# Score visits that own two pairs of PSUM banks instead of four adjacent ones, with a new fixed list

## The chip, the cores and the metric

The kernel runs on one core of one Trainium2 chip. A core has five engines with a queue each: TensorE (PE, matrix products into PSUM), ScalarE (ACT), VectorE (DVE), GpSimd (POOL) and SyncE (SP, which here only issues DMAs). The metric is the device time of one execution in microseconds; the profile is of one execution.

## The reference

The reference is one transformer block on 2048 tokens of 640 features, in bf16: an attention with a compressive memory, then a SiLU feed-forward of width 1728, both behind a LayerNorm without weights and with a residual. The attention has 32 heads of 20 features and works through four segments of 512 tokens:

```python
for s in range(N):                      # N = 4 segments, H = 32 heads
    logits = einsum('bhqd,bhkd->bhqk', qs, ks) * scale + mask      # causal
    a_dot = einsum('bhqk,bhkd->bhqd', softmax(logits), vs)
    pq = phi(qs)                        # t + 1 for t > 0, else exp(t)
    a_mem = einsum('bhld,bhde->bhle', pq, M) / (einsum('bhld,bhd->bhl', pq, z) + 1e-06)
    outs.append(g * a_mem + (1.0 - g) * a_dot)      # g = sigmoid(beta)
    M = M + einsum('bhld,bhle->bhde', phi(ks), vs)
    z = z + sum(phi(ks))
h  = x + concat(outs) @ wo
h2 = h + silu(layernorm(h) @ w1) @ w2
```

## The kernel before

**Tasks and a written list.** The kernel declares some 1,370 small tasks (a group of matmuls into PSUM, an eviction, an exponential, a DMA) with what each reads and writes. `ORDER` (L358) is one fixed list of all of them. `Graph.schedule` (L287) walks it and emits each task on its engine's queue in that order. An entry is `name/engine:slots`: the letter after the slash chooses ACT (A), DVE (D) or SP (S) where a task may run on more than one, and the numbers after the colon are the buffers that the task takes into use. `schedule` refuses a list in which a buffer is taken before its former owner's last user stands in the list. Every engine works strictly through its own part of the list. `Tracker.add` (L79) derives the semaphore waits from the data, so the list sets order and place, and the waits set the times. `fillN` entries are N matmuls on zeros.

**The names.** By segment s, head group g (4 heads, 8 groups), projection chunk c and token block b (128 tokens):
- `n1_st`, `n1_rs`, `n1_ap`, `n1_tr`: LayerNorm of a block (DVE statistics, POOL, DVE apply, DMA transpose issued by SP). The first four blocks are transposed on PE instead (`n1_tp`, evicted by `n1_te`).
- `re_wq`, `re_wk`: the loaded wq and wk are rearranged in SBUF by ACT or DVE.
- `v`, `ve`: value projection (L774) and eviction. `pr`, `qe`: projection of q or k (L808) and eviction. `ex`, `ph`: the two halves of phi. `vt`: twelve small DMAs of a segment that copy parts of q and k to other partitions (L844); the groups 5 to 7 need all of them.
- `qk`: the scores of one visit (L880), `e`: their exponentials (L891), `mk`: causal masks on POOL (L903), `av`: product with the values (L926), `oe`: its eviction (L939, L941), `tn`, `nm`, `ad`: transpose back together with the memory's term, normalisation on DVE, and sum of both parts on POOL.
- `kt`, `mz`, `ma`, `mb`: update of the memory M. `ot`, `wo`, `rs`: transpose of the attention's output by DMA, output projection (L1109), residual. `n2_*`: the second LayerNorm. `h1`, `th`, `s`: first feed-forward product (L1143; the last, narrow one L1138), tanh on ACT, product on DVE. `h2`, `o`, `out`: second product (L1178), residual, store.

The segments overlap: feed-forward and output work of one segment stand in the list among the scores of the next. PE's tasks use three tilings of the array: full, four row tiles (`qk`) and four column tiles (`av`; two in the narrow `h1`).

**PSUM.** The pool `ps` has the eight PSUM banks. A projection or `h1` takes one, a `v`, `wo`, `h2` or memory `tn` two neighbours. A score visit computes four heads at once, one bank each: 512, 384 or 256 + 256 columns. It takes four adjacent banks as one buffer, and two exponentials evict it, each two banks. The four banks come free together in the list, after the second exponential. In the list of before all visits use banks 4 to 7 or banks 0 to 3. The first matmul of a visit waits for everything that the visit needs.

Of the kernel before, what the change touches and what calls it, by code (L numbers as in the profile page):

```python
# [324 lines left out]
D = 640  # L325
# [38 lines left out]
pr020:2 ex001:0 qe021/A:0 e0x2:1 e0x0 qe020/A n1_st5:4 n1_st6:5 pr041:0 re_wq3/D av1x:3 qk2x0:4 w_wo/S:0  # L364
x8/A:8,9,10,11 vt06:0 vt00 vt03 vt09 qe041/D:0 pr031:1 pr030:0 n1_st4:6 n1_st7:7 w_w1_0/A:0 mk0x e2x2:0 oe1x/D:0
e2x0 ex041:1 qe030/D:0 qk0yb0:4 pr040:2 w_w1_1/S qe031/A qe040/D mk2x e0yb2:0 e0yb0 n1_rs5 av2x:0 av0x:3 tn1x:1
nm1x:0,0 oe0x/A:1 mk0yb n1_rs6 mtb1 qk1yb0:4 vt010 oe2x/D:0 vt08 vt05 vt02 vt07 vt04 e1yb2:1 e1yb0 ex021:2 zf0 v03:2
# [12 lines left out]
pr111:0 qe121/D:0 e6ya0:0 e6ya2 qk6yb0:4 qe120/D ex121:2 av5y:3 n2_tr0 h1_0_7_0:1 h1_0_0_0:2 e6yb2:0 e6yb0 qk7ya0:4  # L380
th0_7_0:0 ph101:2 qe111/D:0 oe5y/D:0 tn4y:0 s0_7_0:0 th0_0_0:1 h1_0_8_0:3 nm4y:0 s0_0_0 mz01:1 mz04:0 ma01/D:2
h1_0_3_0:2 e7ya2:1 e7ya0 th0_8_0:0 ma04/D:3 s0_8_0 th0_3_0:1 s0_3_0 tn5y:1 qk7yb0:4 e7yb2:1 mk6yb e7yb0 mk7yb mta0
av6y:0 mtb0 oe6y/A:1 h1_0_12_0:3 h1_0_1_0:2 qk8a0:4 th0_1_0:0 e8a2:0 e8a0 th0_12_0:1 s0_1_0 pr110:0 nm5y:1 qe110/D
h1_0_10_0:2 av7y:1 qk8e0:4 oe7y/D:0 th0_10_0:0 s0_12_0 pr130:0 s0_10_0 e8e2:0 e8e0 h1_0_5_0:2 h1_0_11_0:3 qk8b0:4
th0_5_0:1 n1_ap8:3 qe130/D:0 th0_11_0:0 w_w2_2/S kt03:1 tn7y:0 s0_5_0 nm7y:2 mz03:1 s0_11_0 h1_0_2_0:2 e8b2:0 e8b0
ma03/D:4 h1_0_6_0:0 th0_2_0:1 h1_0_13_0:1 th0_13_0:0 qk9a0:4 pr131:3 s0_2_0 s0_13_0 n1_ap10:0 h1_0_4_0:1 h1_0_9_0:2
qe131/D e9a2:1 e9a0 mk8a mk8e mm0 th0_6_0:1 th0_4_0:0 ex100:1 s0_6_0 mm4 mk8b mm6 qk9b0:4 vt19:0 th0_9_0:1 mm2 mm8
n1_rs9 mtb2 s0_4_0 w_w2_3/S vt16 vt10 vt18 e9b2:1 e9b0 av8:3 h2_0_0:0 h2_0_1 qk10a0:4 s0_9_0 ph100:0 ex141:1 ph121:1
e10a2:0 e10a0 h2_0_2 tn6y:2 h2_0_3 ph141:0 ex120:2 mk9a qk10b0:4 oe8/D:0 nm6y:3 o0 mzc0 mzc6 ph120:0 mzc2 h2_1_0:2
mk9b mm10 mzc4 e10b0:0 kt10:0 vt15 mm1 mzc1 mb00:0 e10b2 mk10a mzc5 mzc8 mm7 mzc7 mb03:0 mk10b ex111:1 n1_tr10:0  # L390
tn8:0 vt11 n1_tr8 nm8:0,0 h2_1_1 vt13 ot2 ot3 qk10e0:4 ph111:2 vt111 kt12:1 vt17 vt110 vt12 h2_1_2 av9:0 h2_1_3
# [24 lines left out]
n1_rs12 n1_ap12:2 ma23 n1_st13:6 e20e2:0 e20e0 th1_7_0:0 h1_1_11_0:2 qk21a0:4 h1_1_5_0:3 ad16 n1_rs14 mk20a s1_7_0
n1_ap14:1 s1_2_0 h1_1_6_0:1 e21a0:1 e21a2 n1_rs13 th1_11_0:0 mk20e n1_ap13:0 mk21a n1_tr12:0 v30:4 n1_tr13 n1_tr14
# [36 lines left out]
def build(nc, es, A_x, A_wq, A_wk, A_wv, A_wo, A_beta, B_x, B_w1, B_w2, out):  # L454
    T = Tracker()
# [396 lines left out]
    def declare_ticks(s):  # L852
# [10 lines left out]
        def scores(name, pool, pt, blocks, pr, width=L, sub=WH):  # L863
# [392 lines left out]
```

## Time and profile before

| what | value |
|---|---|
| median of 3 runs | 306.86 us (306.14 to 307.66) |
| profiled execution | span 305.4 us, its only time on record; the median is 1.46 us above it |
| instructions | 7240 |
| busy PE / ACT / DVE / POOL | 291.0 / 227.0 / 218.7 / 143.5 us |
| exponentials of scores (L891) | 168, 156.2 us busy between 19 and 250 us |
| ACT idle before L891, waiting for L880 | 14.3 us in 25 places |
| mean granted clock of TensorE | 0.994 |

An engine that is busy for the largest share need not be the one that sets the end in every stretch. The kernel has three: a start that waits for weights (to about 18 us), the attention's segments with everything else woven in (to about 250 us), and a tail of feed-forward products (to the end). A line of a group gives source line, engine, operation, tiles, shapes and count, then busy time and mean, then the idle time just before it and what ended that. `SPq` or `ACTq` is that engine's queue issuing a DMA, `PEld` the loading of a matmul's stationary operand.

### The profile page before, as it was taken

What the parts mean: (1) busy time and instruction counts of PE and PEld (TensorE: products, weight loads), DVE (VectorE), ACT (ScalarE), POOL (GpSimd) and SP (SyncE); (2) the same over time, 40 slices, a digit from 0 to 9 for tenths busy, and PEclk for the clock granted to TensorE, in tenths of its full rate; (3) what the DMA queues carried; (4) which work ended last, traced back from release to release, by engine and by line L of the source; (5) the groups of instructions that cost most, each with busy time, mean ns of one, the idle gap of its engine ahead of it and who ended that gap; (6) DMA issues with size and microseconds to landing.
All of it is one profiled execution on the core that took longest, in us unless ns stands there. A gap on an engine that the chain in (4) does not pass through costs nothing.

```text
span 305.4 us, 7240 instructions
## 1 busy us (share of the span) xinstructions
PE 291.0 (95%) x2876; PEld 166.5 (55%) x2900; DVE 218.7 (72%) x490; ACT 227.0 (74%) x322; POOL 143.5 (47%) x280
## 2 busy tenths in 40 slices
PE   8699898999999999999999999999999999999996
PEld 6434454555655445656654444556564466764574
DVE  5567999796788895877989878449776476934523
ACT  4488998999998979989889899978878951004410
POOL 4227754433687856536747419334973730300000
PEclk9899999999999999999999999999999999999999
DMA  6658468642264040055552400034250004242001
GB/s 197 211 195 239 75 166 223 127 97 42 90 105 80 17 62 2 1 91 76 114 146 63 67 17 19 2 64 69 39 108 2 0 2 88 64 88 86 0 24 64
DMA packets 48578, 24.65 MB, mean 81 GB/s; under 512 B 38881, under 2 KB 47457, under 8 KB 48545
## 3 DMA queue, kind: packets, MB, share of 16 engines
q1 hardware_dynamic: 47872, 23.09, 33.1%
q10 hardware_dynamic: 672, 1.10, 1.1%
q8 instruction: 23, 0.38, 0.5%
q14 instruction: 11, 0.08, 0.1%
HBM read 10.41 MB, written 2.62 MB: 43 GB/s over the span
## 4 chain that ended last, share of the span: by engine, by line
PE 72%; ACT 12%; DVE 7%; DMA 4%; issue 2%; POOL 1%; SPq 1%; DVEq 0%; ACTq 0%
PE ps_all L1178 18%; PE ps_all L1143 16%; PE ps_all L808 12%; PE ps_all L1109 7%; PE ps_all L880 6%; PE ps_all L926 5%; ACT PTA L891 4%; ACT PTB L891 3%; DMA sT<-in_A_wq_dram 3%; PE ps_all L774 2%; PE ps_all L955 2%; ACT PTE L891 2%; DMA oT<-otok 1%; PE ps_all L959 1%; PE ps_all L1048 1%
## 5 line engine op out<-in xcount | busy, mean ns | idle before, releaser
L891 ACT ACTIVATE PTA<-ps_all 128x1024 bf16<-128x1024 f32 x64 | 62.1, 1027 | 7.1 <-PE ps_all L880 6.5
L1178 PE MATMUL ps_all<-w_sb,sT 128*128 128x320 bf16 x448 | 65.2, 299 | 0.0
L891 ACT ACTIVATE PTB<-ps_all 128x1024 bf16<-128x1024 f32 (+1 forms) x64 | 58.9, 970 | 5.9 <-PE ps_all L880 5.6
L1143 PE MATMUL ps_all<-hT,w_sb 128*128 128x512 bf16 (+1 forms) x315 | 60.1, 335 | 0.9 <-issue 0.5
L1152 ACT ACTIVATE th<-ps_all 128x512 f32<-128x512 f32 (+2 forms) x70 | 34.0, 507 | 34.5 <-PE ps_all L1143 26.8
L1158 DVE SCALAR_TENSOR_TENSOR sT<-th,ps_all 128x512 bf16<-128x512 f32 (+2 forms) x70 | 38.0, 561 | 26.1 <-ACT th L1152 25.0
L903 POOL TENSOR_SCALAR_AFFINE_SELECT PTB<-PTB 128x512 bf16<-128x512 bf16 x64 | 41.2, 644 | 32.7 <-ACT PTB L891 30.4
L1178 PEld LDWEIGHTS ps_all<-w_sb,sT 128*128 128x128 bf16 x448 | 42.3, 98 | 19.3 <-issue 2.1
L1143 PEld LDWEIGHTS ps_all<-hT,w_sb 128*128 128x128 bf16 x325 | 30.3, 98 | 23.9 <-issue 1.3
L891 ACT ACTIVATE PTE<-ps_all 128x1024 bf16<-128x1024 f32 (+1 forms) x40 | 35.4, 943 | 2.2 <-PE ps_all L880 2.1
L903 POOL TENSOR_SCALAR_AFFINE_SELECT PTE<-PTE 128x512 bf16<-128x512 bf16 x40 | 25.9, 647 | 21.0 <-ACT PTE L891 19.5
L706 DVE BATCH_NORM_STATS2 stt<-x_tok 128x6 f32<-128x320 bf16 x64 | 27.9, 477 | 1.5 <-DMA x_tok<-in_A_x_dram 1.3
L808 PE MATMUL ps_all<-xT,wqr 128*128 128x512 bf16 x92 | 24.3, 391 | 3.2 <-ACT xT L741 2.4
L1109 PE MATMUL ps_all<-wo_sb,oT 128*128 128x320 bf16 x160 | 24.1, 299 | 1.0 <-DMA oT<-otok 0.7
L774 PE MATMUL ps_all<-wv_sb,xT 128*128 128x320 bf16 x160 | 24.3, 300 | 0.7 <-DMA xT<-xn_rot 0.5
L808 PE MATMUL ps_all<-xT,wkr 128*128 128x512 bf16 x94 | 24.0, 386 | 0.5 <-issue 0.3
L1000 POOL TENSOR_TENSOR otok<-on 128x320 bf16<-128x320 bf16 x24 | 19.0, 792 | 11.3 <-DVE on L992 11.3
L903 POOL TENSOR_SCALAR_AFFINE_SELECT PTA<-PTA 128x512 bf16<-128x512 bf16 x24 | 15.5, 645 | 16.6 <-ACT PTA L891 16.4
L1195 DVE SCALAR_TENSOR_TENSOR x_tok<-ps_all,x_tok 128x640 bf16<-128x640 f32 (+1 forms) x17 | 13.2, 780 | 14.1 <-PE ps_all L1178 14.0
L880 PE MATMUL ps_all<-QK 20*128 20x256 bf16 (+3 forms) x360 | 20.5, 286 | 1.7 <-ACT PTB L891 0.7
L992 DVE TENSOR_TENSOR on<-ps_all,rd 128x640 bf16<-128x640 f32 x24 | 19.8, 825 | 0.8
L817 DVE CAST QK<-ps_all 128x512 bf16<-128x512 f32 x24 | 16.3, 687 | 5.5 <-PE ps_all L808 5.1
(79 smaller groups left out, 403.5 us busy)
## 6 DMA issues: line engine op xcount, KB each, us to landing
out_dram<-x_tok SPq DMA_DIRECT2D x15, 160.0 KB, 1.9
w_sb<-in_B_w_dram SPq DMA_DIRECT2D x4, 432.0 KB, 5.8
w_sb<-in_B_w_dram SPq DMA_DIRECT2D x3, 480.0 KB, 4.3
x_tok<-in_A_x_dram SPq DMA_DIRECT2D x2, 640.0 KB, 4.7
QKV<-QK SPq DMA_DIRECT2D x16, 72.0 KB
wv_sb<-in_A_wv_dram SPq DMA_DIRECT2D x1, 800.0 KB, 4.9
sT<-in_A_wq_dram SPq DMA_DIRECT2D x1, 800.0 KB, 8.2
sT<-in_A_wk_dram SPq DMA_DIRECT2D x1, 800.0 KB, 9.9
```

Source lines behind the costliest of these rows:

```text
L706: T.add(DV, lambda e, hh=hh: e.bn_stats(out=stt[:, s, 6 * hh:6 * hh + 6], in_=xb[:, 320 * hh:320 * hh + 320]), reads=R((xa, xsub)), writes ...
L774: fns.append(lambda e, c=c, hh=hh: e.matmul(bank(ps, hh)[:, 0:320], lhsT=xT[:, c, 128 * i:128 * i + 128], rhs=wv_sb[:, c, 320 * hh:320 * h ...
L808: fns = [lambda e, kc=kc: e.matmul(bank(ps)[:, lo:hi], lhsT=wt[:, kc, c, :], rhs=xT[:, kc, lo:hi], start=(kc == 0), stop=(kc == NC - 1)) f ...
L880: fns.append(lambda e, j=j, o=o, r=r, q0=q0, q1=q1, qa=qa, ka=ka: e.matmul(ps_all[:, o:o + q1 - q0], lhsT=ka[32 * r:32 * r + DH, 128 * j:1 ...
L891: T.add(AC, lambda e: e.activation(out=pt[:, pta.slot, q0:q0 + 2, 0:width], in_=sc3[:, b0:b0 + 2, 0:width], func=ACT.Exp, scale=SCALE), re ...
L903: fns.append(lambda e, v=v: e.affine_select(out=v, in_=v, pattern=[[0, 4], [1, 128]], compare_op=ALU.is_ge, fill=0.0, base=0, channel_mult ...
L992: T.add(DV, lambda e: e.tensor_tensor(out=on[:, ona.slot, :, :].rearrange("p b (x e) -> p b x e", e=DH), in0=v[:, :, :, 0:DH], in1=r2.unsq ...
L1109: fns.append(lambda e, c=c, hh=hh: e.matmul(bank(ps, hh)[:, 0:320], lhsT=oT[:, c, 128 * i:128 * i + 128], rhs=wo_sb[:, c, 320 * hh:320 * h ...
L1143: fns = [lambda e, c=c: e.matmul(bank(ps)[:, lo:hi], lhsT=w1_sb[:, c, 128 * f:128 * f + 128], rhs=hT[:, c, lo:hi], start=(c == 0), stop=(c ...
L1152: T.add(AC, lambda e: e.activation(out=th[:, tha.slot, lo:hi], in_=bank(ps)[:, lo:hi], func=ACT.Tanh, scale=0.5), reads=R((ps, [0])), writ ...
L1158: T.add(DV, lambda e: e.scalar_tensor_tensor(out=sT[:, f, lo:hi], in0=th[:, tha.slot, lo:hi], scalar=1.0, in1=bank(ps)[:, lo:hi], op0=ALU. ...
L1178: fns.append(lambda e, f=f, t0=t0, fr=fr, hh=hh: e.matmul(bank(ps, hh)[:, 0:320], lhsT=sT[:, f, t0:t0 + 128], rhs=w2_sb[:, fr, 320 * hh:32 ...
```

## The change

A visit now allocates two buffers of two banks, `sca[0]` for heads 0 and 1 and `sca[1]` for heads 2 and 3, which may lie anywhere, also on odd banks and in either order. Each is read by one exponential and comes free with it, so the list may give one pair to another task, or to the next visit, while the other is still to be evicted. The visit itself is still one group of matmuls, whose first one waits for both pairs; the instructions are the same. A `qk` entry carries two numbers now. The list is new from end to end: same 1,371 entries in another order, with 42 tasks on another engine (the most of them between ACT and DVE, and the loads x8, w_w1_0 and w_w2_4 between ACT's and SP's queue) and other buffers.

```diff
 ORDER = """
-zpad:0 x0:0 x1:1 w_wv:0 x2:2 x3:3 beta w_q:0 w_k halfc warm:0 iota vpad0 sel n1_st0:0 n1_st1:1 epsc mt3 vpad1 n1_rs0
-n1_rs1 epsg0 n1_ap0:0 fill21:0 n1_tp0:0 n1_te0/A:0 n1_ap1:1 fill6:2 n1_tp1:2 n1_te1/A v00:0 v01:2 n1_st2:2 n1_rs2
-n1_st3:3 n1_rs3 mt1 mt2 mta1 n1_ap2:2 n1_ap3:3 n1_tp2:4 n1_te2/D re_wq1/A:0 fill4:6 n1_tp3:6 n1_te3/A pr010:6
-re_wk1/D:0 re_wk0/D re_wk3/D x4/S:4,5,6,7 pr011:4 re_wk2/D re_wq4/D qe011/D:0 ve00/A:0 re_wk4/A qe010/A re_wq2/A
-lsc0 pr001:0 ve01/D lsc1 lsc2 re_wq0/A qe001/A:0 qk1x0:4 e1x2:0 pr000:1 qe000/D lsc3 pr021:0 e1x0 mk1x qk0x0:4
...
-qk3x0:4 v02:0 e3x0:0 e3x2 n1_ap6:0 n1_ap5:1 ve03/D n1_tr5:0 vt011 vt01 qk4x0:4 ve02/D tn0x:2 e4x2:1 nm0x:1 e4x0 mm5
...
-e6x0:1 e6x2 tn4x:3 oe0y/D:0 av5x:0 tn3x:1 oe5x/A:1 qk7x0:4 e7x2:0 e7x0 nm4x:3 v10:2 nm3x:0 qk2ya0:4 ph041:2
...
+iota:0 x0:0 sel zpad fill4:6 epsc fill21:0 warm:0 n1_st0:6 x1:1 fill6:2 halfc n1_st1:5 n1_rs0 n1_ap0:3 n1_tp0:0
+n1_te0/A:0 x2:2 w_wv:0 x3:3 n1_rs1 n1_ap1:2 n1_tp1:2 n1_te1/A n1_st2:1 mt3 n1_st3:7 w_q:0 n1_rs2 mt0 n1_rs3 w_k
+n1_ap2:0 n1_ap3:3 re_wq3/D:0 v00:0 beta ve00/A:0 re_wq1/A v01:6 n1_tp2:3 n1_tp3:0 n1_te3/D n1_te2/D pr010:1 re_wk0/D:0
+ve01/D re_wq0/D re_wq2/A x4/S:4,5,6,7 pr001:0 re_wk3/D re_wk1/A pr011:6 w_w2_4/A w_w2_3/S mt1 vpad1 qe010/D:0 pr000:1
+qe011/A qe001/D:0 ex001:0 re_wk2/D re_wk4/D w_w1_2/S:0 ph001:1 lsc0 zf0 qk1x0:5,3 mta0 vpad0 pr021:2 e1x0:0 mtb0
...
+w_w1_4/S vt06:0 ex021:1 re_wq4/D lsc1 lsc2 n1_st7:2 zf1 vt03 pr030:5 mk0x pr031:4 e2x0:0 e2x2 mk2x w_wo/S:0 lsc3
+oe1x/A:1 qk0yb0:1,6 qe041/A:0 pr040:3 vt09 mm4 mzc4 n1_ap5:3 e0yb0:0 mta3 e0yb2 n1_st6:5 n1_rs6 av2x:2 av0x:1 qe040/A
+mtb1 mm3 x8/S:8,9,10,11 qe030/D:0 qe031/D qk1yb0:6,4 e1yb2:1 e1yb0 oe2x/D:0 mk0yb ph021:0 tn1x:0 ex031:0 v03:2 vt00
+qk3x0:4,6 e3x2:0 nm1x:1,0 oe0x/D:1 v02:0 e3x0 ve03/D qk4x0:6,2 n1_ap6:1 e4x0:1 n1_tr5:0 e4x2 vt08 mk3x vt07 fill4:5
...
@@ scores
-                sca = G.alloc("ps", nr)
-
-                def e_qk(eng, sca=sca, r0=r0, nr=nr):
+                sca = [G.alloc("ps", 2) for _ in range(nr // 2)]
+                scw = [(a, [0]) for a in sca]
+
+                def e_qk(eng, sca=sca, scw=scw, r0=r0, nr=nr):
...
-                            o = 512 * (sca.slot + r - r0) + co
+                            o = 512 * (sca[(r - r0) // 2].slot + (r - r0) % 2) + co
...
-                    T.run(PE, fns, R(*ra), R((sca, [0])))
-                G.task(f"qk{name}{r0}", {PE: width / 2400.0 + 0.012 * len(blocks)}, e_qk, ra, [(sca, [0])],
+                    T.run(PE, fns, R(*ra), R(*scw))
+                G.task(f"qk{name}{r0}", {PE: width / 2400.0 + 0.012 * len(blocks)}, e_qk, ra, scw,
...
-                    def e_ex(eng, q0=q0, r0=r0, sca=sca):
-                        b0 = sca.slot + q0 - r0
+                    scp = sca[(q0 - r0) // 2]
+
+                    def e_ex(eng, q0=q0, scp=scp):
+                        b0 = scp.slot
...
-                    G.task(f"e{name}{q0}", {AC: act_c(2 * width)}, e_ex, [(sca, [0])], [(pta, [q0])],
+                    G.task(f"e{name}{q0}", {AC: act_c(2 * width)}, e_ex, [(scp, [0])], [(pta, [q0])],
```

More of the change, by code (lines that the diff above doesn't have):

```diff
@@ L364 @@
[L364 to L367, printed above, removed]
-qk3x0:4 v02:0 e3x0:0 e3x2 n1_ap6:0 n1_ap5:1 ve03/D n1_tr5:0 vt011 vt01 qk4x0:4 ve02/D tn0x:2 e4x2:1 nm0x:1 e4x0 mm5
@@ L449 @@
-out7 h2_14_2 h2_12_0:6 h2_14_3 out10 out9 out8 out4 h2_15_0:0 o14 out14 h2_15_1 h2_15_2 h2_15_3 h2_12_1 h2_12_2 o15
-h2_12_3 out15 o12 h2_13_2 h2_13_3_0 out12 o13_0 out13_0 h2_13_3_1 o13_1 out13_1
+iota:0 x0:0 sel zpad fill4:6 epsc fill21:0 warm:0 n1_st0:6 x1:1 fill6:2 halfc n1_st1:5 n1_rs0 n1_ap0:3 n1_tp0:0
+n1_te0/A:0 x2:2 w_wv:0 x3:3 n1_rs1 n1_ap1:2 n1_tp1:2 n1_te1/A n1_st2:1 mt3 n1_st3:7 w_q:0 n1_rs2 mt0 n1_rs3 w_k
+n1_ap2:0 n1_ap3:3 re_wq3/D:0 v00:0 beta ve00/A:0 re_wq1/A v01:6 n1_tp2:3 n1_tp3:0 n1_te3/D n1_te2/A pr010:1 re_wk0/D:0
@@ new lines @@
+mtb1 mm3 x8/S:8,9,10,11 qe030/D:0 qe031/D qk1yb0:6,4 e1yb2:1 e1yb0 oe2x/D:0 mk0yb ph021:0 tn1x:0 ex031:0 v03:2 vt00
+qk3x0:4,6 e3x2:0 nm1x:1,0 oe0x/D:1 v02:0 e3x0 ve03/D qk4x0:6,2 n1_ap6:1 e4x0:1 n1_tr5:0 e4x2 vt08 mk3x vt07 fill4:5
+ve02/D qk0ya0:4,0 e0ya0:0 tn2x:7 vt011 vt02 n1_st4:5 nm2x:1 tn0x:2 nm0x:2 n1_st9:6 mk4x fill6:3 av3x:3 oe3x/D:1 vt05
+mzc2 qk1ya0:6,4 mk1yb av4x:2 oe4x/D:0 n1_rs4 e0ya2 v11:0 n1_tr6 vt01 ve11/D:1 tn4x:2 n1_rs7 n1_ap4:3 n1_ap7:1 vt010
+nm4x:0 vt04 av0y:3 e1ya0:1 e1ya2 qk5x0:6,4 mm0 v12:0 w_w2_2/S oe0y/A:0 n1_tr4 e5x0:0 qk6x0:2,6 e5x2 mk5x ve12/D tn3x:0
@@ new lines @@
+h2_1_3 o1 qk11a0:0,4 e11a0:1 ph111:1 wo3:6 av10:2 vt10 kt10:0 e11a2 qk11b0:4,0 mb01:0 rs3 n1_rs11 vt14 oe10/D:0 tn9:6
+mk11a wo2:2 nm9:0,0 ex131:2 rs2 e11b0:0 qk12a0:6,4 e11b2 mk11b v20:0 e12a0:0 n2_st2:7 n1_ap11:3 av11:2 mzc7 e12a2
+ve20/A:0 oe11/D:1 vt15 vt11 vt110 n2_rs2 vt13 qk13a0:4,6 kt12:1 mz12:3 e13a0:1 e13a2 v21:0 ma12 qk12b0:4,2 n2_st3:4
+n1_tr11 mz10:6 ad9:0 n2_rs3 e12b0:1 mm8 ve21/D n2_ap2:2 ma10 pr210:7 ph131:0 tn10:0 e12b2 qk12e0:5,3 ex141:1 mzc8
+mb03:0 nm10:0,0 mk12a pr231:2 pr220:0 e12e2:1 mk12b e12e0 ad10 qe210/D:0 qe231/D:0 n2_ap3:3 qk13b0:4,2 mm10 e13b0:0
@@ new lines @@
+ex201:0 s0_4_1 qk16b0:2,0 e16b2:0 av15:7 nm12:1,0 pr240:5 oe15/D:0 tn15:0 out1 ad14 th0_12_1:1 s0_12_1 e16b0
+qk16a0:2,6 pr230:4 ex210:2 qe240/A h1_0_6_1:5 e16a2:0 h1_0_0_1:6 nm15:1,1 e16a0 th0_6_1:1 ad12 h1_0_13_1:0 th0_13_1:0
+ad15 ph201:0 qe230/D vt24:0 ot6:0 s0_6_1 mk16b th0_0_1:1 mk16a h1_0_10_1:7 qk16e0:2,4 s0_13_1 th0_10_1:0 ph210:0
+e16e0:0 ot7 e16e2 mk16e v22:0 s0_0_1 h1_0_11_1:6 th0_11_1:1 s0_10_1 h1_0_5_1:7 th0_5_1:0 ve22/D qk17b0:2,0 e17b2:1
+s0_5_1 wo6:4 e17b0 s0_11_1 av16:6 rs6 vt20 n2_st6:7 ot4 mk17b qk18b0:0,2 oe16/A:0 n2_rs6 e18b0:0 mb13:0 wo7:4 rs7
```

149 lines of the change are left out of this document (70 added, 79 removed).

## The prediction

> **What bounds the kernel now.** I read the busy shares first, then the slices, then stretches of time, then the chain that ended last, and at the end the groups and the waits.
>
> ```profile
> PE 291.0 (95%) x2876; PEld 166.5 (55%) x2900; DVE 218.7 (72%) x490; ACT 227.0 (74%) x322; POOL 143.5 (47%) x280
> ...
> PE   8699898999999999999999999999999999999996
> ...
> ACT  4488998999998979989889899978878951004410
> ```
>
> TensorE (PE) is busy for 95% of the span, but a busy PE may be waiting inside its pipeline, so I split its time by the starts of its matmuls. In the trace a 512-column matmul starts 216 ns after the one before, a 320-column one 136 ns, a 256-column one 109 ns: columns / 2.4 + 2.5 ns. Four row or column tiles start 3 to 5 ns apart and cost one of them. Where the tiling changes (full array to the row tiles of L880 or the column tiles of L926 and back) some 95 ns come on top: 229 ns instead of 136. The list's matmuls cost 261.8 us this way and its 217 tiling changes 20.6 us, 282.4 in all. The last group starts at 302.05 us, where the work ahead of it is 281.9: PE has slipped by 20.1 us. The slip, start minus work ahead, is 6.6 us at the first projection (13.8 us), 7.8 at the first scores (18.3), 12.6 at 52.8, 13.6 at 81.6 and 20.1 at 250.9; after that it stands still. Only the slip can be won.
>
> ```profile
> 11.00:19.00 8.00, 5.62 (x29) 2.33 (x31) 3.99 (x16) 5.69 (x15) 0.26 (x1) 0.79 0.56 186
> ...
> 34.00:39.00 5.00, 4.02 (x51) 2.15 (x52) 4.50 (x13) 5.00 (x7) 3.11 (x5) 1.00 0.52 79
> 39.00:44.00 5.00, 4.44 (x67) 2.46 (x66) 4.67 (x15) 4.84 (x8) 2.36 (x7) 1.00 0.62 139
> 44.00:49.00 5.00, 4.26 (x74) 2.43 (x76) 4.51 (x14) 4.34 (x7) 4.07 (x8) 1.00 1.06 339
> ```
>
> Columns: stretch, its length, busy us of PE, weight loads, DVE, ACT and POOL (instructions), granted clock, DMA share, GB/s. The slip grows fastest from 18 to 53 us (by 4.8), and there ACT is full (5.00 of 5, 4.84 of 5), DVE nearly so, PE not. The chain of that stretch:
>
> ```profile
> 42.51 1.43 ACT PTE L891 x2
> ...
> 43.98 0.43 PE ps_all L880 x8
> 44.41 0.02 issue
> 44.43 1.95 ACT PTA L891 x2
> 46.38 0.05 issue
> 46.43 0.37 PE ps_all L880 x8
> 46.80 0.02 issue
> 46.82 1.52 ACT PTB L891 x2
> 48.34 0.04 issue
> 48.39 0.40 PE ps_all L880 x8
> ```
>
> Two exponentials, then the scores that need their four banks, then two exponentials: each pass leaves ACT without work for the 0.4 us of the scores (its longest are 0.50 at 44.43 and 0.45 at 51.23). The same ring shows in the whole kernel's waits:
>
> ```profile
> PEld ps_all L880 <- ACT PTB L891: 6.8, 20, 0.8
> ACT PTA L891 <- PE ps_all L880: 6.5, 11, 0.9
> PEld ps_all L880 <- ACT PTA L891: 4.0, 13, 0.4
> ```
>
> The PEld times hold 0.26 us each that every start of a row-tiled group shows, whoever released it. Added up by starts, PE slips 2.5 us at score groups, 1.9 of it before 60 us. So the ring costs PE little by itself; ACT's total load in 18 to 53 us costs more.
>
> **The change part by part.** *PE's work.* The same matmuls in nearly the old order; counted through the new list, 216 tiling changes for 217: -0.1 us (bounds -0.1 and 0).
>
> *The banks.* I went through both lists and asked for each of the 84 visits which exponential last frees its banks, and what ACT has queued between that one and the visit's own first exponential. Before: 17 visits have nothing there, one has another exponential. After: 5 have nothing, 28 still have an exponential of the previous visit running (0.81 to 1.02 us by its rows), which covers the 0.4 us of the scores. Of the six visits that close the ring between 31 and 53 us four are covered so: qk4x, qk2ya, qk3ya, qk4ya.
>
> *ACT's load.* From the first exponential to qk3ya (18.9 to 48.4 us) the old list gives ACT 26.3 us of work at the back-to-back spacings of the trace (0.905 for 1024 columns, 0.70 for 768, 0.50 for an eviction), the new one 23.9: four evictions more go to DVE than come back, one exponential and one of phi's come later. DVE's load in the same stretch falls too, 24.6 to 22.1, because LayerNorm statistics of later blocks move behind it. Up to av8 (81.6 us) it is 59.0 to 56.3 on ACT, 50.4 to 51.9 on DVE. Ends: all of both effects, 2.4 + 4 x 0.43 = -4.1, nearly the 4.8 of slip; or nothing, if another queue binds at the same place. SP does nearly: qk5x needs twelve copies (vt, L844) that SP issues from 23.5 to 35.6 with hardly a gap; they have landed at 37.41, 0.6 ahead of qk5x.
>
> ```profile
> 23.52 4.07 SPq L844 DMA_DIRECT2D QKV<-QK  x4
> 27.63 0.51 SPq L565 DMA_DIRECT2D w_sb<-in_B_w_dram  x1
> 28.48 4.18 SPq L844 DMA_DIRECT2D QKV<-QK  x6
> 32.71 1.32 SPq L747 DMA_TRANSPOSE xT<-xn_rot  x1
> 34.09 1.46 SPq L844 DMA_DIRECT2D QKV<-QK  x2
> ```
>
> In the new list SP's run from the first copy to the last also holds w_wo, x8 (both formerly elsewhere) and two transposes, n1_tr5 and n1_tr6: by the issue rows (0.64 to 0.91 a copy, 1.2 to 1.3 a transpose, 0.4 to 0.5 a load) 11.8 us against 12.0. The last copy lands near 37.2, so up to qk5x, which stands 0.5 later in PE's work, 1.2 us of slip can go; I take 0.9 (the transpose for v11, which slips 0.59 waiting for it, is now ahead of six copies). From qk5x to 52.8 the slip grew by 2.6, and three covered visits lie there (3 x 0.43 = 1.3); I take 1.1. Together -2.0, the middle of the ends.
>
> *Later.* The largest single slips after 60 us are wo6 0.80 (behind the transpose of otok), av19 0.64 and wo2 0.45. The new list has 0.5 us more PE work between pr230, whose eviction SP's queue waits for ahead of that transpose, and wo6. I take -0.5; ends 0 and -1.9.
>
> *The new waits.* A score group now often takes a pair that somebody else used: 56 visits instead of 7 need DVE's or another eviction's release besides exponentials, and all that follows on PE's queue waits too. The trace shows a separate wait instruction of 51 ns ahead of 23 of the L880 matmuls; the seven visits that had such a release slipped 0.13 at most, 0.01 in the middle. Ends 0 and 49 x 0.051 = +2.5; I take +0.3, since the queue ahead of PE hides most of them.
>
> *The start.* zpad now stands behind iota (0.23) and sel (0.78), so the warm-up matmuls start near 2.1, not 1.12, and all 31 precede the first transpose instead of 21: at 213 ns until the clock rises at 6.4 and 109 after, that transpose comes near 7.6, not 5.69. It is covered: PE idles 2.6 us until 13.77 for the weights (landed 11.87). But both last xT evictions now queue on DVE behind re_wq3: 11.87 + 0.45 + 0.72 + 0.80 = 13.85 instead of 13.31; against that w_q is issued 0.47 earlier, beta now behind it. The first scores come one projection later (1.08 us) on PE. Taken: +0.2; ends -1.4 and +1.7, by the clock.
>
> The clock first by rows: PE pauses from 11.2 to 13.8, is granted 0.79 of its clock over 11 to 19, and starts 512-column matmuls 427 ns apart until 16.3; that is 1.4 us of slip. My sum leaves it in, since the pause stays above 2 us. The Trainium skill, TensorE: Matmul & The Clock Gate, section Why this matters for your kernels, asks only that no gap exceed some 3 us; by it neither pause would halve the clock and the sum would be 1.4 lower. This trace disagrees: 2.6 us were enough.
>
> Sum: -0.1 - 2.0 - 0.5 + 0.3 + 0.2 = -2.1 on the profiled span of 305.4, 303.3; the median of 306.86 lies 1.46 above that span, so 304.8 us.
>
> **The rivals.**
> - *Another queue takes ACT's place.* For: DVE is 4.50 and 4.67 busy of 5 where ACT is full, SP issues without a gap; 58 of the 84 visits still take four adjacent banks, and 5 + 21 have less than 0.65 us of cover, so the change does only part of what it says. Against: DVE's load falls as well. The stretch then gives 0.5: 306.3.
> - *The joint waits end last.* A visit's first matmul waits for the later of an exponential and an eviction, and PE cannot pass it. Against: the seven cases above. For: DVE is nearly full where most of the 49 new ones lie. At 0.05 us a visit it eats the forecast's gain (2.4 without the +0.3); at 0.1 it costs 4.9: 309.4. It decides slower from 0.08, (2.4 + 1.5) / 49.
> - *The clock is not halved.* If the later warm-up shortens the pause enough: 304.8 - 1.4 = 303.4. For: the pause shrinks, to some 2.1 by the start's sum. Against: 2.6 sufficed. The rule of the Trainium skill above would give this time.
>
> **How the numbers follow.** Forecast 0.42, another queue 0.26, joint waits 0.24, clock 0.08. Three runs spread by 0.25% around their median, so a measurement tells about 0.5% (1.5 us) from no change: faster is under 305.3, slower over 308.4. Faster 0.47 (forecast less a small part above 305.3, and the clock case), same 0.29, slower 0.24. The forecast's own range is 302.5 to 305.5; over all cases 301.8 (4.1 of the stretch and 1.4 later) to 309.2 (joint waits of 0.096).
>
> **What would show it.** Right: between 34 and 49 us ACT's busy share falls and PE's rises; in the chain the scores no longer stand between pairs of exponentials; the slip at 52.8 us of old time is 2 less and that lasts to 250. The idle time before L891 for L880 falls from 14.3 us. Wrong: waits of L880 for DVE lines (x_tok, oTs, rd) above 2 us in all; DVE or SP full at 25 to 40; first projection after 14.8; more than 3.4 us at half clock. What would break the prediction most is a slip from 60 to 250 us that grows by more than the old 7.2, for then the won time is given back.

## The result and the profile after

The changed kernel takes 310.52 us, median of four executions (309.91 to 311.35), the kernel before 306.5 (305.69 to 307.66): a ratio of 1.0139, 95% interval 1.0105 to 1.0173. By the ratio it is slower by some 4.3 us. The profiled execution, the slowest of the four, has a span of 309.6 us.

The page of the kernel after, busy shares and slices:

```profile
PE 290.1 (94%) x2876; PEld 165.8 (54%) x2900; DVE 225.2 (73%) x501; ACT 223.6 (72%) x311; POOL 143.4 (46%) x280
...
PE   7699789999999999999997999999989998999996
...
ACT  4569799899999889999897888878869951004500
```

The work is the same; PE now has three slices under 9 between 160 and 265 us, where before it had none. The stretches that the prediction showed, now after (length, then busy us of PE, weight loads, DVE, ACT, POOL, and the granted clock):

```profile
11.00:19.00 8.00, 6.49 (x47) 3.26 (x46) 6.75 (x23) 4.87 (x13) 2.56 (x9) 1.00 0.60 185
...
34.00:39.00 5.00, 3.80 (x58) 2.37 (x59) 3.43 (x10) 3.56 (x5) 3.35 (x9) 1.00 0.49 101
39.00:44.00 5.00, 4.17 (x53) 2.10 (x52) 3.58 (x7) 4.64 (x8) 3.40 (x6) 1.00 1.02 214
44.00:49.00 5.00, 4.51 (x69) 2.35 (x68) 2.94 (x11) 4.96 (x7) 2.92 (x9) 1.00 0.39 26
```

The clock is full at the start. From 34 to 44 us ACT and DVE are less busy than before, and PE is less busy too: neither of them held it. The slip (start minus work ahead, as in the prediction) says when it was lost:

| slip of PE at | before | after |
|---|---|---|
| first scores, qk1x (18 us) | 7.75 | 6.64 |
| qk5ya (56 us) | 12.85 | 12.38 |
| h1_0_8_1 (117 us) | 15.61 | 15.86 |
| h1_1_11 (166 us) | 18.25 | 19.47 |
| qk28b (221 us) | 19.30 | 21.13 |
| h1_2_12 (251 us) | 20.10 | 23.43 |
| last group | 20.15 | 24.48 |

At 117 us the two are level, but only because the profile of before ran at half clock from 13.2 to 16.6 us and that of after did not: from the first scores to 117 us the new list slips 9.2 us and the old one 7.9. That half clock is not the rule. In the experiments below 12 of the 76 executions of the kernel before show a mean granted clock of 0.994 or less, and by the medians those take 2.0 to 2.5 us longer than the others beside them. Most of the loss is made behind 117 us: PE slips 8.6 us there where it slipped 4.5.

To see by what, I took for every group of matmuls the slip that it adds and PE never recovers, and looked for the last of its needs to end within 0.6 us of its start: an input, or the last reader of the group that had its banks before. Behind the first scores that gives (good to some 0.3 us for a row, since some matmul records are missing from the traces):

| what the group waited for last | before | after |
|---|---|---|
| a visit, for an exponential that frees its banks | 3.44 | 1.40 |
| a visit, for another eviction that frees its banks | 0.23 | 2.75 |
| another group, for an exponential that frees its banks | 0.48 | 2.25 |
| any group, for a DMA to land | 1.41 | 4.85 |
| everything else | 6.96 | 6.53 |

The ring of scores and exponentials did open, by 2.0 us. Against it stand 2.5 at visits that wait for evictions, 1.8 at other groups that were given a bank of a visit, and 3.4 at DMAs (mz23 1.70, qk5x 1.21, wo14 1.00, mz01 0.48 and h1_2_4 0.38 are most of the 4.85). The waits of the scores (line L880, now L881) show the exchange. In the view of that line, what its engine sat idle for (us, times), first before:

```profile
  ACT PTB L891: 7.5, 22
  ACT PTE L891: 4.3, 14
  ACT PTA L891: 4.2, 14
  issue: 4.1, 16
```

And after:

```profile
  issue: 6.8, 20
  ACT PTB L894: 3.8, 12
  ACT PTA L894: 3.0, 10
  DVE x_tok L1198: 2.2, 3
  ACT PTE L894: 1.6, 5
  DVE on L995: 1.5, 5
  ACT th L1155: 1.2, 3
  DVE Vx L785: 1.0, 3
```

Before, no DVE row was over 0.4 there. The longest of the new ones is qk29b at 228.6 us. Weight loads of PE, then DVE, at that place:

```profile
226.54 0.93 PEld L1181 LDWEIGHTS ps_all<-w_sb,sT 128*128 128x128 bf16 x8 [0.47 <-DVE oTs L944]
228.63 0.12 PEld L881 LDWEIGHTS ps_all<-QKV 20*128 20x128 bf16 x8 [1.15 <-DVE x_tok L1198]
```

```profile
225.75 0.74 DVE L944 TENSOR_SCALAR oTs<-ps_all,lsc 128x512 bf16<-128x512 f32 x1
226.41 0.66 DVE L830 TENSOR_SCALAR phiQ<-QK 128x512 bf16<-128x512 bf16 x1
227.11 0.73 DVE L833 TENSOR_TENSOR phiQ<-phiQ,ex 128x512 bf16<-128x512 bf16 x1
227.76 0.81 DVE L1198 SCALAR_TENSOR_TENSOR x_tok<-ps_all,x_tok 128x640 bf16<-128x640 f32 x1
```

The visit took the banks of h2_6, whose residual o6 (L1198) stands behind oe26 and the two halves of ph320 on DVE. The largest DMA wait is mz23 at 164.5 us; PE's weight loads, then SP's queue:

```profile
164.51 0.33 PEld L1051 LDWEIGHTS ps_all<-Vx,phiKt 128*128 128x128 bf16 x4 [2.03 <-DMA phiKt<-phiK]
```

```profile
154.99 0.82 SPq L1203 DMA_DIRECT2D out_dram<-x_tok  x2
159.36 0.40 SPq L562 DMA_DIRECT2D x_tok<-in_A_x_dram  x1
159.81 1.20 SPq L1043 DMA_TRANSPOSE phiKt<-phiK  x1
```

SP waits from 155.8 to 159.36, until the store out2 has landed and the load x12 may overwrite its buffer. The transpose kt23 that mz23 needs stands behind that load. In the old list it stood ahead of both and was issued at 151.59.

### The profile page after: what moved, and what is told of

Read it like the earlier page. It is cut to its first block, busy times and chain, and to the rows that moved or that the text cites. A ratio compares the mean times of both kernels' runs of the same rounds, so it can differ in the third digit from the quotient of the medians.

```text
span 309.6 us, 7286 instructions
## 1 busy us (share of the span) xinstructions
PE 290.1 (94%) x2876; PEld 165.8 (54%) x2900; DVE 225.2 (73%) x501; ACT 223.6 (72%) x311; POOL 143.4 (46%) x280
## 4 chain that ended last, share of the span: by engine, by line
PE 63%; DVE 17%; DMA 10%; issue 3%; ACT 2%; POOL 1%; SPq 1%
PE ps_all L1146 14%; PE ps_all L1181 14%; PE ps_all L808 9%; PE ps_all L1112 6%; PE ps_all L774 6%; PE ps_all L881 5%; PE ps_all L929 4%; DMA x_tok<-in_A_x_dram 4%; DVE stt L706 3%; DMA phiKt<-phiK 3%; DVE QK L817 2%; DVE on L995 2%; PE ps_all L958 2%; PE ps_all L1051 1%; PE ps_all L962 1%
## 5 line engine op out<-in xcount | busy, mean ns | idle before, releaser
L1181 PE MATMUL ps_all<-w_sb,sT 128*128 128x320 bf16 x448 | 64.2, 299 | 0.1
L1198 DVE SCALAR_TENSOR_TENSOR x_tok<-ps_all,x_tok 128x640 bf16<-128x640 f32 (+1 forms) x17 | 13.2, 781 | 20.3 <-PE ps_all L1181 20.2
L808 PE MATMUL ps_all<-xT,wkr 128*128 128x512 bf16 x93 | 23.1, 380 | 0.8 <-issue 0.7
L881 PE MATMUL ps_all<-QK 20*128 20x256 bf16 (+3 forms) x360 | 20.6, 285 | 1.4 <-DVE on L995 0.3
L817 DVE CAST QK<-ps_all 128x512 bf16<-128x512 f32 x30 | 20.0, 678 | 1.8 <-PE ps_all L808 1.6
L715 POOL TENSOR_TENSOR rst<-mvt,eps_c 128x1 f32<-128x1 f32 x32 | 6.5, 203 | 31.1 <-DVE mvt L709 31.1
```

Source lines behind the costliest of these rows:

```text
L808: fns = [lambda e, kc=kc: e.matmul(bank(ps)[:, lo:hi], lhsT=wt[:, kc, c, :], rhs=xT[:, kc, lo:hi], start=(kc == 0), stop=(kc == NC - 1)) f ...
L817: (lambda e: e.tensor_copy(out=o, in_=i_))
L881: fns.append(lambda e, j=j, o=o, r=r, q0=q0, q1=q1, qa=qa, ka=ka: e.matmul(ps_all[:, o:o + q1 - q0], lhsT=ka[32 * r:32 * r + DH, 128 * j:1 ...
L1181: fns.append(lambda e, f=f, t0=t0, fr=fr, hh=hh: e.matmul(bank(ps, hh)[:, 0:320], lhsT=sT[:, f, t0:t0 + 128], rhs=w2_sb[:, fr, 320 * hh:32 ...
```

## The experiments

Ratios are against the kernel before, run in turn with each kernel on the same chip, with the 95% interval. Executions of one kernel spread by 1.4 to 4.4 us, and a profile is one of them; so I trust a wait when it returns in several profiles, and a time by its interval.

**The code without the list.**

```diff
-qk1x0:4
+qk1x0:4,6
...
-qk3x0:4
+qk3x0:4,6
...
```

> The new code with the old list: every visit owns two pairs, but takes them next to each other, on the banks that it had before. Theory A (the new list puts the inputs of PE late in the queues of SP and DVE; owning pairs costs nothing by itself): the same as before, 306.5 us, within 0.5 us, and a slip of PE of 20 us at the end. Theory B (pairs cost by themselves, since a visit's first matmul now waits for two buffers): above before by 84 visits x 0.03 to 0.05 us = 2.5 to 4.2 us, 309 to 310.7, and a slip of 22.5 or more.

306.07 us, ratio 1.0019 (0.9995 to 1.0043), slip 20.3 at the end. Owning pairs costs nothing that can be measured. The change is its list.

**Which half of the list.** Both halves can be joined: at the 617th entry (118 us) the lists have done the same tasks but for three.

The new list's first 617 entries, then what is left in the old list's order and on its engines; one buffer has another number. The seam:

```diff
 ma13 n2_tr2 h1_0_7_1:2
-th0_7_1:0 qk14e0:0,6 e14e2:1 e14e0 kt11:1 ph141:1
+ph141:0 kt11:0 qe221/A qk14e0:4,6 th0_7_1:0 s0_7_1
```

> The new list up to its 617th entry (about 117 us), then everything that is left in the old list's order, on the old engines. By both lists nearly the same tasks are done there (8 stand on different sides), and PE's slip is 15.9 (new) and 15.7 (old). Theory A (the loss comes from the order of the new list's second half): PE slips 4.4 to 5 us from there, as before, and the time is that of before, 305.7 to 306.5 us (ratio 0.997 to 1.003). Theory B (the first half leaves the second with queues that stand later, and the old order would lose there too): 309 to 310.5 us.

307.03 us, ratio 1.0015 (0.9989 to 1.0040). Six of the 24 executions of the kernel before beside it show a granted clock of 0.994 or less, and none of its own twelve does; against the other 18 (median 306.0) it is 1.0 us slower. The reverse is the old list's first 618 entries and then the new order, with five buffers renamed; its seam:

```diff
 pr221:2 h1_0_7_1:3 oe13/D:1 ma13 ph140:0 mk14a
+th0_7_1:0 qk14e0:0,6 e14e2:1 e14e0 mk14b kt14:1
```

> The old list up to its 618th entry (about 117 us), then what is left in the new list's order. Theory A: PE slips some 8.5 us from there, as in the changed kernel, and the time is 309.5 to 310.5 us (ratio 1.012 to 1.016). Theory B: 306 to 307 us.

309.58 us, ratio 1.0105 (1.0066 to 1.0143), and 3.6 us slower than the same 18. From h1_0_8_1 to the end PE slips 7.5 us there and 4.8 in the run above; the kernel before had 4.5, the changed one 8.6. The three waits of the new order are there again, with the old one ahead of them; weight loads of the run with the old list first:

```profile
162.78 0.22 PEld L1051 LDWEIGHTS ps_all<-Vx,phiKt 128*128 128x128 bf16 x3 [1.93 <-DMA phiKt<-phiK]
...
187.17 0.19 PEld L958 LDWEIGHTS ps_all<-Mzb,phiQ 128*128 128x128 bf16 x4 [0.84 <-DVE phiQ L833]
...
226.91 0.12 PEld L881 LDWEIGHTS ps_all<-QKV 20*128 20x128 bf16 x8 [1.15 <-DVE x_tok L1198]
```

So most of the loss belongs to the order of the second half, not to what the first half leaves behind; about 1 us is the first half's own.

**Two cuts further on.** The new list to its 926th entry (172 us) and to its 1142nd (229 us), then the old order; the seams:

```diff
 n1_tr15 pr330:7 ph211:2
-qe330/D:0 e22b2 mk22b qk23a0:1,4
+kt21:0 ad18 e22b2 ex241:2 th1_8_0:0 qk23a0:4,1
...
 o6 qk29b0:4,0 e29b2:0 e29b0
-tn27:2 mk29b n2_ap8:2 h2_7_1
+kt22:1 n2_ap8:1 tn27:4 h2_7_1
```

> The new list up to its 926th entry (about 172 us), then the old order. Up to the 617th entry the new list costs nothing (ratio 1.0015). If the loss is made by late inputs one at a time, this one holds the loss of 118 to 172 us alone: mz23 behind the load x12 (0.5 to 1.7 by four profiles) and qk20b behind nm17 (0.44), less av19 of the old order (0.64) = 0.3 to 1.5 us over the list cut at 117: ratio 1.003 to 1.006. If the loss is made at the end of the list: 1.0015 as there.

310.96 us, 1.0155 (1.0113 to 1.0197).

> The new list up to its 1142nd entry (about 229 us), then the old order. It adds tn20 behind ph240 (0.65), h2_7 behind oe26 (0.32) and qk29b behind o6 (0.90) to the list cut at 172 us: 1.9 us more than that one, ratio 1.008 to 1.012; what is then left to the changed kernel's 1.014 is wo14 and h1_2_4 (0.84 + 0.38). If those waits only show a lateness that the earlier part makes: no more than the list cut at 172 us.

313.51 us, 1.0228 (1.0183 to 1.0273). Neither is faster than the changed kernel itself, and each loses time at its seam: right behind the first cut pr310 slips 2.1 us for a bank that an exponential still holds, and right behind the second tn27 does (2.1). Behind that second seam the clock is halved for 3.4 us (qk29a slips 0.8, h2_7_3 0.5), and all six executions of that list show a granted clock of 0.995; of the list cut at 172 us four of six show 0.994 or 0.995. The cuts settle nothing more than the halves did. They do show what a bank costs that a visit has handed over too late.

**Late inputs moved forward.** First two that touch no visit:

```diff
-th1_12_0:1 x12/S kt23:0 mz23:3
+th1_12_0:1 kt23:0 x12/S mz23:3
-qk24e0:6,4 ve33/D th1_3_0:1 ph240:0
+qk24e0:6,4 ph240:0 ve33/D th1_3_0:1
```

> The changed kernel with two tasks moved in the list that touch no visit: kt23 ahead of x12 in SP's queue, ph240 ahead of ve33 in DVE's. Theory A: mz23 slips 0.3 instead of 1.7 (its transpose is issued at 158.5 instead of 159.8) and tn20 0 instead of 0.65; together 2.0 less, and that stays to the end: 308.5 us. Theory B (visits that wait for a release by DVE set the pace of the late segments): the slips turn up again at the visits behind, 310.5 us and a slip of 24 or more at the end.

309.44 us, 1.0119 (1.0090 to 1.0149). In its profile both slips are gone, mz23's and tn20's; the time is some 0.6 us lower, which the intervals do not tell from nothing. That profile has other waits in their place: h1_0_8_1 2.0 us (a transpose, kt11, landed 4.4 us after its issue, and ph141 on DVE waited for it with an eviction behind it) and h1_1_11 1.2. Then the one visit:

```diff
-h2_6_3 ph320:0 n2_tr9:0 e28e2 mk28e h2_7_0:6 o6 qk29b0:4,0
+h2_6_3 o6 ph320:0 n2_tr9:0 e28e2 mk28e h2_7_0:6 qk29b0:4,0
```

> The changed kernel with the residual o6 ahead of ph320 in DVE's queue. o6 frees a pair that visit qk29b takes; in the changed kernel o6 ends at 228.57 and the visit starts at 228.63, 0.90 late. If that joint wait costs what it shows: o6 ends near 227.3, the visit slips 0.1 instead of 0.9, and the time is 0.8 lower, 309.7 us. Rival: the visit is only where the waiting shows, another input (tn27 or h2_7 behind it) is as late, and nothing is won: 310.5 us.

310.05 us, 1.0136 (1.0103 to 1.0169). qk29b no longer slips, qk29a behind it slips 0.54, and h1_2_4 0.85 where it had 0.38: the time is what the rival said, and not to be told from the changed kernel's. Together, with n2_ap8 moved ahead of ph320 too:

```diff
-ph320:0 n2_tr9:0 e28e2 mk28e h2_7_0:6 o6 qk29b0:4,0
+o6 n2_ap8:1 ph320:0 n2_tr9:0 e28e2 mk28e h2_7_0:6 qk29b0:4,0
...
```

> The changed kernel with five tasks moved in their queues, all after 155 us and none of PE's or of its banks: kt23 ahead of x12 on SP, ph240 ahead of ve33, o6 and n2_ap8 ahead of ph320 on DVE. If the late inputs are the cause and each wait can be taken away by itself: 1.2 + 0.65 + 0.8 + 0.2 = 2.8 us less than the changed kernel, ratio 1.004 to 1.006. If taking one away shows the next (as the other banks did): less than half of it, ratio above 1.009.

308.76 us, 1.0095 (1.0067 to 1.0122): by the ratios 1.4 us less than the changed kernel, half of what the waits add up to, and the two intervals overlap. What is left after the moves shows at h1_2_4, whose transpose is now the last to come:

```profile
231.22 0.76 PEld L1146 LDWEIGHTS ps_all<-hT,w_sb 128*128 128x128 bf16 x5 [1.05 <-DMA hT<-xn_rot]
```

**The copies on SP at 22 to 38 us.** The prediction had PE gain there. The last of SP's run in the changed kernel, with the transpose n1_tr6 among the copies:

```profile
28.18 3.58 SPq L844 DMA_DIRECT2D QKV<-QK  x5
31.87 2.24 SPq L747 DMA_TRANSPOSE xT<-xn_rot  x1
34.16 2.03 SPq L844 DMA_DIRECT2D QKV<-QK  x3
```

The edit:

```diff
-e2x2 mk2x w_wo/S:0 lsc3 oe1x/A:1
+e2x2 mk2x lsc3 oe1x/A:1
...
-v11:0 n1_tr6 vt01 ve11/D:1 tn4x:2 n1_rs7 n1_ap4:3 n1_ap7:1 vt010 nm4x:0 vt04 av0y:3
+v11:0 vt01 vt010 vt04 w_wo/S:0 n1_tr6 ve11/D:1 tn4x:2 n1_rs7 n1_ap4:3 n1_ap7:1 nm4x:0 av0y:3
```

> The changed kernel with the last three of the twelve copies (vt) ahead of the transpose n1_tr6 in SP's queue, and the load of w_wo behind them. In the changed kernel qk5x slips 1.2 us (0.9 and 1.0 in two other profiles), released by the last copy. Theory A (SP's queue has taken ACT's place there): the last copy is issued 2.8 us earlier, qk5x slips 0.1 to 0.2, the slip at 53 us falls by 0.8 to 1.2 and the time by as much, to 309.3 us. Rival: DVE and ACT are as late there (tn0x, tn3x and the next evictions take over, or v12 waits for the later transpose): the slip at 53 us stays within 0.3 and the time at 310.3 us.

313.59 us, 1.0221 (1.0169 to 1.0272), 2.5 us slower than the changed kernel. qk5x slips nothing; v12 behind it slips 2.8, for the transpose that was put back:

```profile
36.39 0.12 PEld L881 LDWEIGHTS ps_all<-QKV 20*128 20x128 bf16 x8 [0.16 <-issue]
39.45 0.52 PEld L774 LDWEIGHTS ps_all<-wv_sb,xT 128*128 128x128 bf16 x5 [2.95 <-DMA xT<-xn_rot]
```

With either order PE's longest wait in this stretch is for SP's queue, for whichever of its DMAs comes last.

**Other banks, same order on every engine.** In the changed kernel, the groups that wait for a bank get one that had come free by then:

```diff
-tn0x:2
+tn0x:6
...
-tn3x:0
+tn3x:4
...
-qk3ya0:6,4
+qk3ya0:0,4
...
-qk29b0:4,0
+qk29b0:0,6
...
```

> The changed kernel with the same order on every engine and other PSUM banks for 70 of the list's buffers: where the profile shows PE waiting for a bank (tn0x, tn3x, qk3ya, qk4yb, tn7x, qk29b, tn29 and others), the group takes one that has been free by then. Theory B2 (the pairs as this list places them cost: 2.7 us of slip at visits that wait for an eviction and 2.3 at other groups that wait for an exponential, against 0.2 and 0.5 before): most of 0.7 + 0.3 + 0.4 + 0.9 + 0.2 goes, 2 to 2.5 us, 308 us (ratio 1.005 to 1.008). Theory A (the queues of SP and DVE alone): the waits come back at the next late copy or eviction, 310 us (ratio 1.013).

312.96 us, 1.0227 (1.0183 to 1.0270). The waits were dealt out anew, and to worse places:

```profile
228.23 0.12 PEld L881 LDWEIGHTS ps_all<-QKV 20*128 20x128 bf16 x8 [0.26 <-ACT PTE L894]
229.33 0.19 PEld L958 LDWEIGHTS ps_all<-Mzb,phiQ 128*128 128x128 bf16 x4 [0.98 <-DVE x_tok L1198]
```

The visit qk29b starts without a wait; the group behind it, tn27, took the banks that o6 frees and waits 0.8 us for the same eviction. The same choice on the old list, for 45 buffers, is the bank part of the change without its order:

```diff
-qk2ya0:4
+qk2ya0:0,6
...
-qk3ya0:4
+qk3ya0:6,0
...
-av3x:4
+av3x:7
...
```

> The old list, the same order on every engine, with the new code and other banks for 45 buffers: a visit takes the pairs that came free first, wherever they lie (qk2ya, qk2yb, qk3ya, qk4ya, qk4yb, qk7ya among them). This is the bank part of the change alone. If it does what it says: the slip of visits that wait for an exponential, 2.2 us between 19 and 60 us, falls to about 1, that of av3x (0.46) goes, and 1.0 to 1.5 us stays won: 305 us (ratio 0.995 to 0.997). Rival: ACT and DVE are full there, what the visits win is lost at the next group that needs an exponential: ratio 0.999 to 1.002.

310.04 us, 1.0123 (1.0080 to 1.0165). Between 19 and 60 us the visits' slip for exponentials falls from 2.2 to 1.2 and av3x's goes, as expected, and more than that comes back: other groups' slip for evictions rises from 0.8 to 2.7 (the fills 0.64, wo1 0.59, pr101 0.40) and for DMAs from 0.6 to 1.7. These banks were my choice, by the times of one profile; that no choice would win is not shown. Both moves in SP's and DVE's queues together with the other banks:

> The changed kernel with the other banks of the first of these runs and two tasks moved in the queues (kt23 ahead of x12 on SP, ph240 ahead of ve33 on DVE). If banks and queues together are the loss: 2 to 2.5 us from the banks, 1.1 to 1.4 from kt23 and 0.65 from ph240, 306.3 us (ratio 1.000 to 1.003); what is left of the loss is wo14 (0.85) and the copies before qk5x. If only one of the two is: 308 to 309 us.

312.10 us, 1.0184 (1.0145 to 1.0224), above both forecasts.

**The start.** More matmuls on zeros ahead of the last transpose:

```diff
-fill4:6 n1_tp3:6
+fill16:6 n1_tp3:6
```

> The kernel before with fill16 for fill4 ahead of n1_tp3: 12 more matmuls on zeros, 12 x 109 ns = 1.3 us, so that PE pauses from 12.5 to 13.8 us instead of 11.2 to 13.8. If a pause of 1.3 us leaves the clock at 1.0, as the changed kernel's start (pause 12.7 to 14.1) has it: no half clock at 13 to 16.6 us, 1.1 to 1.4 less slip at the first scores, and 305.1 to 305.4 us if PE keeps it to the end. Rival: the scores from 18 to 53 us wait for the copies on SP or for ACT anyway, and the gain is given back there as in the changed kernel (slip 12.9 at 60 us as before): 306.5 us.

307.50 us, 1.0056 (1.0030 to 1.0082). The clock stays at 1.00, but the fills push the transpose, its eviction and with it the first projection, to 14.9 us. Behind the transpose, on a free bank, in the old order with other banks:

```diff
 fill4:6 n1_tp3:6
+fill12:4
 re_wq1/A:0 n1_te3/A
```

> The kernel of the run before it, with twelve more matmuls on zeros (fill12) behind n1_tp3, on a bank that is free there, so that PE pauses some 1.2 us shorter ahead of the first projection, without anything standing later. If the pause halves the clock in that kernel and no longer here: no granted clock of 0.5 at 13 to 17 us, and up to 1.3 us less: 304 us (ratio 0.991 to 0.994). Rival: the pause halves the clock in some executions only, and the first projection waits for the fills in those whose weights land early: no difference to the run before it.

309.41 us, 1.0117 (1.0075 to 1.0159), as without them (1.0123). The clock was full in both profiles; four of the six executions without the fills and two of the six with them show 0.994. The new list's first 100 entries with the old list behind them:

> The new list up to its 100th entry (about 22 us), then the old one. The start of the changed kernel slipped 1.1 us less up to 19 us in the profile shown (5.2 and 5.8 in two others, against 7.6), since the clock is not halved. Theory A: the win of the start stays, since nothing in the old list from 22 to 60 us has to wait longer: 304.3 to 305.4 us (ratio 0.994 to 0.998). Rival: the copies on SP's queue and ACT's load set the pace from 22 to 53 us whatever the start is, and the slip at 53 us is 12.5 again: 306.5 us (ratio 1.000).

308.10 us, 1.0041 (1.0009 to 1.0074): pr040 slips 2.2 us for a bank whose eviction, oe1x, stands behind two statistics on DVE at the seam. Eight of its twelve executions show a granted clock of 0.994 (median 308.2 us), the other four, the profiled one among them, 1.00 (306.4). With these behind it:

```diff
-lsc3 n1_st6:5 w_wo/S:0
+lsc3 w_wo/S:0
...
-pr030:5 n1_st4:6 w_w1_0/A mk0x e2x2:0 oe1x/D:0 e2x0
+pr030:5 w_w1_0/A mk0x e2x2:0 oe1x/D:0 n1_st6:5 n1_st4:6 e2x0
```

> The new list up to its 100th entry, then the old one, as tried before, with the statistics n1_st6 and n1_st4 behind oe1x in DVE's queue; in that earlier run they stood ahead of it, and pr040 slipped 2.2 us for the bank that oe1x frees. Without this the start's win stays to the end: slip of 17.5 to 18 at the end, ratio 0.995 to 0.998, and less than both kernels. Rival: the copies and ACT from 22 to 53 us take it back, ratio 1.000 to 1.004.

306.27 us, 1.0001 (0.9977 to 1.0025). The same as before; no run here beats the kernel before.

## Why the prediction was wrong

It forecast 304.8 and at most 309.2, with 0.24 for slower, and named the right event as what would break it most: a slip from 60 to 250 us that grows by more than 7.2. It grew by 11.0. In the slips of the two profiles its sum of -2.1 reads +4.3: the work -0.1 as forecast, the start -1.1 for +0.2, from the first scores to 60 us +0.7 for -2.0, and behind that +4.8 for -0.5, with the new waits (+0.3) spread over both. Step by step:

- **PE's work, -0.1.** Right: the slip and the span account for the times with it.
- **The banks.** Right in what it says of exponentials. Of the four visits named, qk4x, qk2ya and qk4ya, which slipped 0.31, 0.23 and 0.13, slip 0.01 at most, and qk3ya 0.29 for 0.55. The row fell by 2.0 us over the whole kernel, more than the 1.1 taken.
- **The stretch 18 to 53, -2.0.** Wrong in both of its terms; ACT's load fell as forecast, but it had not been the limit. Up to qk5x 0.9 was to be won, and PE slips 2.75 us from the first scores to there where it had 2.24. The step that failed here is SP's run of copies: 11.8 us by the sum, 14.0 in the trace (22.15 to 36.19), because n1_tr6 took 2.24 us of the queue, not 1.2 to 1.3, and because the sum left out the time between the issues, 1.0 us in all. So the last copy landed near 37.9, not 37.2, and qk5x slipped 1.2. From qk5x on 1.1 was to be won, and PE slips 2.99 us to qk5ya where it had 2.86, though no group there loses time to a DMA. Counted as in the table above, from the first scores to 60 us visits wait 1.5 us less for exponentials, and PE's groups 1.9 more for banks and 0.6 more for DMAs. So the rival "another queue takes ACT's place" came true, with SP as the queue, but the banks given from one owner to the next took back more than SP did.
- **Later, -0.5.** The largest error, shown by the two halves: the step that failed most is the order of the queues behind 60 us, which the sum took as harmless. I asked of the three largest old slips whether they would go, and two did (wo6 0.80 and av19 0.64 are not in the new profile). I did not go through the new list behind 60 us for what it would make late: kt23 behind x12 (1.7), o6 behind ph320 (0.9), ph240 behind ve33 (0.65; ve33 had come from ACT), ot14 for wo14 (1.00). For SP's queue I did that work for one stretch only.
- **The new waits, +0.3.** Mis-sized: visits slip 2.5 us more for evictions, the upper end of the range given (+2.5). 32 visits have such a release last, but eight make most of it, qk29b, qk20b and qk4yb 1.7 of it. The separate wait instructions ahead of the scores went only from 23 to 29, 0.3 us at 51 ns each; what cost more was that the evictions ended late. The seven cases of the old list, where the queue hid it, were no sample of these. And the other direction was not in the sum at all: a bank that a visit hands over makes its taker wait for an exponential, 1.8 us more (tn0x alone 0.57).
- **The start, +0.2.** Wrong in sign: -1.1 in this profile. The last eviction of xT ended when forecast (13.71 for 13.85), but the first transpose came at 6.66, not 7.6, and the clock was not halved. The pause ahead of the projection, read as 2.6 us and forecast as 2.1, was shorter than the matmul records say, since the record of that projection's first matmul is missing. By the weight loads, before and after, it was 2.20 us from start to start and is 1.23:

```profile
13.36 0.13 PEld L808 LDWEIGHTS ps_all<-xT,wqr 128*128 128x128 bf16 x2 [2.14 <-ACT xT L741]
```

```profile
13.83 0.77 PEld L808 LDWEIGHTS ps_all<-xT,wqr 128*128 128x128 bf16 x5 [1.15 <-ACT xT L741]
```

  The rival "the clock is not halved" had 0.08; it came true, and the half clock that the sum kept is in few executions of the kernel before. The Trainium skill, TensorE: Matmul & The Clock Gate, section Why this matters for your kernels, asks for no gap above some 3 us; here a gap of 1.63 us came just ahead of a half clock in one run, and one of 2.94 us did not in another (last section).
- **The base.** The sum added 1.46 us to the profiled span. Every execution whose own span is on record takes 1.7 or 1.8 us more than that span, so the base was some 0.3 us low.
- **The rival "joint waits end last"** forecast 309.4, nearest to the result, but at 0.1 us for each of 49 visits. It was 0.05, and late DMAs made up the rest.

The profile's signs, as set out ahead: ACT's busy time from 34 to 49 us fell (right), PE's fell with it from 12.7 to 12.5 instead of rising, the slip at 53 us was 0.8 lower and not 2, less than the start had won, ACT's idle time for the scores rose from 14.3 to 19.8 instead of falling, and the scores waited for DVE lines for more than 2 us in all (the rows shown above).

What stays open: the moves in the late queues won 1.4 us of the 4.3, with intervals that overlap, and the bank choices none. That the list and not the code makes the loss, and that the second half's order holds most of it, is shown. That it is the sum of the named waits is not, since each one taken away uncovered part of the next.

## What to carry to other kernels

Where every engine follows one written list, a new list is judged by each queue's order from end to end: for every input of the busiest engine, what now stands ahead of it on the DMA, vector and scalar queues. A wait that a change removes is worth only as much as the next latest input allows, here about half or less. And a bank given out before its reader is done passes the wait on to its next owner: the two choices of banks tried here, with all eight in use, moved the waits and won nothing.

## What the runs showed of the hardware

- A transpose by DMA lands behind the load or store that was issued ahead of it on SP. In all 260 cases of the eighteen profiles in which such a load or store was still in flight when a transpose was issued, the transpose landed at least 0.46 us after it. In seven profiles with x12 ahead, kt23 landed 0.49 to 0.52 us after x12 had (163.94 and 164.46 in the changed kernel), up to 4.7 us after its own issue; in three with the store out2 ahead, 0.52, 0.55 and 0.91 us after that. Over all transposes of a profile the median from issue to landing is 2.65 us, but 13 of 59 (before) and 20 of 59 (after) took over 3.0, some 4.0 to 4.4 with no reason that I found; ot14, for one, 4.2 to 4.4 in nine profiles with the new order or a part of it. A list leaves such landings slack or does not.
- The clock was halved in three of eighteen profiles, for 3.41 us each time: from 13.2 us in the kernel before, from 13.7 in the code alone with the old list, and from 232.2 in the list cut at 229 us:

```profile
232.20:235.60 3.40, 3.40 (x21) 1.60 (x19) 1.37 (x3) 0.84 (x1) 1.06 (x2) 0.50 0.28 56
```

  PE's matmul starts just ahead of these lay 2.20, 1.63 and 2.26 us apart. The length of a gap alone does not decide it: ten gaps of 1.82 to 2.94 us in other places, the longest in the run with the copies first, left the clock at 1.00. With the new list's first 100 entries, whose profile has a gap of 2.29 us at 24 us, eight of twelve executions show 0.994 and four 1.00. What else decides stays open. The old start had gaps of 1.08 and 1.26 us in two other profiles, at full clock, so the clock's win is not the new list's alone.
